# Recurrent attention with a rational feed-forward: the written order of all steps replaced, with some copies, products and half sums on other engines

## The chip, the core and the metric

One core of a Trainium2 chip runs the whole kernel. The metric is device time in microseconds (us) of one execution; lower is better. PE is the matrix engine (TensorE), DVE VectorE, ACT ScalarE, POOL GpSimd, SP the engine that mostly issues transfers. Each engine works through its own queue strictly in the order in which the kernel was written, and waits at an instruction whose inputs or buffers are not ready.

## The reference, cut to what matters

```
f = 1 / (1 + exp(-f_logit))                          # q, k, v, f_logit: 4 x 8 x 768 x 48
for t in range(768):
    state = f[:, :, t, :, None] * state + outer(k[t], v[t])
    y[:, :, t] = q[t] @ state                        # per batch and head
x = y as 3072 tokens x 384
h = x @ w_in                                         # 384 -> 2048
P = a0 + a1 h + a2 h^2 + a3 h^3
Q = 1 + |b0| |h| + |b1| h^2
out = (P / (Q + 1e-6)) @ w_out                       # 2048 -> 384
```

## The kernel before, in words

The 3072 tokens are cut into twelve units of 256 (four batches, three stretches of time). A unit goes through an attention part and a feed-forward part, and several units are under way at once.

Attention part of a unit. `ld` loads f, k, q (SP's queue) and v (POOL's queue). ScalarE takes exp and log of the gate (`ef`, L284; `ls`, L289). PE forms running sums (`cs`, L299 to L308). ScalarE takes their exp, once for q and once for k (`A`, L316), and a short one for the chunk decay (`ae`, L448). `xa` (L321) multiplies q (x = 0) or k (x = 1) with that into `qkp`, on VectorE or, with the letter p, on GpSimd. `T` (L335) transposes the products on PE into PSUM, and `Te` copies them into SBUF as T: on ScalarE with the letter s (L344), read as 1024 words of 32 bits, or on VectorE (L345), as 2048 of 16 bits. `sc` (L357) and `mk` (L365, VectorE) form masked scores; `ic`, `si` and `st` (L422, L432, L452) carry the state on; `yi` and `yb` (L377) form y. `ye` scales y into x, on ScalarE (L440) with a factor held in a register that `fr` (L278) loads, or on VectorE (L442).

Feed-forward part. `h` (L463) is a quarter of x @ w_in, four blocks of 128; `hy` (L480, ScalarE) brings it to SBUF. VectorE forms `sq` (h squared, L484), `ab` (the absolute value, L488), `p1`, `pm`, `p2` (L524, L534, L529). The sum z of the denominator is made by an adding transfer that POOL issues (`zd`, L510), by VectorE (`zv`, L506), or on PE (`u`, L496). The last sum of the numerator, into g, is likewise an adding transfer (`ta`, L538) or a half sum on VectorE (`tv`, L542). ScalarE takes the logarithm of the denominator (`lz` L514, or `ln` L501 out of PSUM) and exp of its negative (`ex`, L519) into qi; `gm` (L546) multiplies that into g; `o` (L555) is a quarter of g @ w_out for 128 tokens; `oe` (L562) copies it out of PSUM on ScalarE or VectorE and `so` (L571) stores it. The two last numbers of a feed-forward step are its range of the 16 blocks of 128.

What sets the order. ORDER (L19 to L94) is a written-out list of all steps; it is walked once, and each step appends its instructions to the queues of its engines. `@0` to `@3` names one of four PSUM slots of two banks each; a new tile in a slot waits until the old one has been read. `!x2` marks a step, and `^x2` lets a later step begin only behind the marked one; the loads of w_in (`wi`, L212) all carry `^w`, the mark of the fifth load of SP's queue, half of unit 0's q. Transfers have eight semaphores per issuing kind, used in turn: the ninth transfer of a kind waits on its queue until the first has landed. v 0 and v 1 are the first two of POOL's, the twelve pieces of w_in follow, so the ninth to the twelfth piece wait for the first to the fourth.

Of the kernel before, what the change touches and what calls it, by code (L numbers as in the profile page):

```python
# [29 lines left out]
yi 1 1 @0; hy 0 12 16; yb 1 2 4; yb 1 0 2; ls 3; ab 0 8 16; u 0 0 4 @3; ef 4; sq 0 8 16; ld 6 f; cs 3 @2; ld 5 f  # L30
ln 0 0 4; p1 0 0 16; T 2 @1; ye 1 s; ae 3; Te 2 s; h 1 4 8 @3; zv 0 8 16; ld 4 k; pm 0 0 16; u 0 4 8 @0; A 3 0
ld 4 q; si 2 0 @1; hy 1 4 8; ic 2; ln 0 4 8; ld 5 q; st 2 0; vm 3; h 1 8 12 @3; ld 4 v; p2 0 0 16; A 3 1; si 2 1
ls 4; sc 2 1 @0; st 2 1; wo 4 8; h 1 0 4 @2; hy 1 8 12; xa 3 0 !x3; ef 5; vm 2; mk 2 1; sc 2 0 @1
# [590 lines left out]
```

## Time and profile before

| what | value |
|---|---|
| three runs | 217.24, 218.63 and 219.75 us, median 218.63 |
| the profiled execution, its whole time | 217.03 us |
| its span, first to last instruction | 215.3 us |
| what lies around the span | 1.73 us |
| granted PE clock, mean | 0.995 |
| DMA queue of POOL / of SP, share of 16 engines | 70.3% / 35.4% |
| transfers, whole kernel | 44.22 MB |

In a row of groups stand line, engine, operation, output and input with their shapes and the count, then busy us and the mean ns of one, then the idle time ahead of them and what ended it. In a row of time stand start, duration, engine, line, operation and count. In a row of waits stand who waited for whom, the us in total, how often and the longest. In a row of stretches stand the stretch, its length and the busy time of each engine with the number of its instructions. Records of neighbouring instructions on one engine overlap a little, so the distance between two starts is shorter than a duration.

### The profile page before, as it was taken

The page shows a single profiled execution, that of the slowest core. Times are in us where ns is not written, and L with a number is a line of the kernel's source. Part 1 is how long each engine was busy: PE and PEld are TensorE (multiplying, and loading weights), DVE is VectorE, ACT ScalarE, POOL GpSimd, SP SyncE. Part 2 cuts the span into 40 slices and gives each one's busy share as a digit, 9 for nine tenths or more (in the row PEclk, how much of TensorE's full clock was granted, in tenths as well). Part 3 has the DMA queues.
Part 4 walks back from the last instruction along what each step waited for, and adds up shares of the span by engine and source line. Part 5 has one row for each costly group of instructions (what it writes and reads, how often), then busy time and mean ns, then how long its engine had stood idle before and what let it go on. Part 6 is the DMA issues. An engine that isn't in the chain of part 4 may idle for free.

```text
span 215.3 us, 6663 instructions
## 1 busy us (share of the span) xinstructions
PE 193.1 (90%) x2931; PEld 139.9 (65%) x2933; DVE 197.4 (92%) x195; ACT 190.1 (88%) x182; POOL 88.5 (41%) x101
## 2 busy tenths in 40 slices
PE   0396799989998999999989999999999999999991
PEld 0374577767874777775876875875885667765550
DVE  3199789999999999999999999999999999999961
ACT  2753499997999899999999999999999899999970
POOL 7174070734935418134447449371155303431100
PEclk9999999999999999999999999999999999999997
DMA  5999999999999999999998999999999998799865
GB/s 140 223 231 213 241 251 225 232 220 254 202 172 201 180 199 219 254 189 258 244 278 192 193 178 202 187 211 208 169 216 204 197 196 191 150 195 195 174 182 146
DMA packets 62557, 44.22 MB, mean 205 GB/s; under 512 B 51520, under 2 KB 57408, under 8 KB 62528
## 3 DMA queue, kind: packets, MB, share of 16 engines
q0 software_dynamic: 21264, 24.91, 70.3%
q1 hardware_dynamic: 40896, 18.78, 35.4%
q8 instruction: 23, 0.38, 0.7%
q10 hardware_dynamic: 368, 0.10, 0.3%
q14 instruction: 6, 0.05, 0.1%
HBM read 25.17 MB, written 4.72 MB: 139 GB/s over the span
## 4 chain that ended last, share of the span: by engine, by line
ACT 26%; PE 26%; DVE 24%; DMA 11%; issue 9%; SPq 1%; ACTq 0%; DVEq 0%
PE op L555 11%; PE hp L463 9%; ACT hy L480 8%; ACT qi L519 8%; DMA w_in_sb<-in_moe_w_in_dram 6%; DVE scm L365 5%; ACT lq L514 5%; DVE h L484 4%; DMA q<-in_q_dram 3%; DVE g L534 3%; PE y L377 3%; DVE z L506 2%; ACT A L316 2%; DMA out_dram<-osb 2%; DVE z L488 2%
## 5 line engine op out<-in xcount | busy, mean ns | idle before, releaser
L463 PE MATMUL hp<-x,w_in_sb 128*128 128x256 bf16 x576 | 68.0, 273 | 2.8 <-DMA w_in_sb<-in_moe_w_in_dram 1.0
L555 PE MATMUL op<-w_out_sb,g 128*128 128x384 bf16 x384 | 68.8, 326 | 0.7 <-ACT hy L480 0.4
L463 PEld LDWEIGHTS <-w_in_sb 128*128 128x128 bf16 x576 | 55.3, 98 | 13.1 <-issue 3.9
L480 ACT CAST hy<-hp 128x1024 bf16<-128x1024 f32 x48 | 48.1, 1046 | 5.0 <-PE hp L463 4.0
L555 PEld LDWEIGHTS <-g 128*128 128x128 bf16 x384 | 36.1, 98 | 23.8 <-issue 1.1
L519 ACT ACTIVATE qi<-lq 128x4096 bf16<-128x4096 f32 (+1 forms) x14 | 44.2, 3172 | 0.0
L514 ACT ACTIVATE lq<-z 128x2048 f32<-128x2048 bf16 x22 | 42.2, 1961 | 0.0
L510 POOL DMA_DIRECT2D z<-h x17 | 18.7, 1155 | 34.7 <-DVE z L488 16.8
L538 POOL DMA_DIRECT2D g<-hy x20 | 19.5, 1012 | 30.9 <-PE hp L463 9.6
L484 DVE TENSOR_TENSOR h<-hy 128x4096 bf16<-128x4096 bf16 (+1 forms) x14 | 29.3, 2090 | 2.5 <-ACT hy L480 2.5
L546 DVE TENSOR_TENSOR g<-g,qi 128x4096 bf16<-128x4096 bf16 (+2 forms) x19 | 28.0, 1496 | 0.9 <-ACT qi L519 0.8
L365 DVE TENSOR_TENSOR scm<-sc,mask 128x1024 bf16<-128x1024 f32 x24 | 28.6, 1211 | 0.0
L534 DVE TENSOR_TENSOR g<-g,h 128x4096 bf16<-128x4096 bf16 (+1 forms) x16 | 28.1, 1768 | 0.0
L316 ACT ACTIVATE A<-cs 128x768 f32<-128x768 f32 (+1 forms) x26 | 19.9, 786 | 1.6 <-PE cs L308 1.5
L321 POOL TENSOR_TENSOR qkp<-q,A 128x768 bf16<-128x768 f32 x7 | 12.7, 1820 | 16.7 <-DMA q<-in_q_dram 7.1
L299 PE MATMUL cs<-lsp,Ui 128*128 128x384 bf16 (+1 forms) x39 | 11.1, 344 | 9.1 <-ACT lsp L289 8.7
L284 ACT ACTIVATE f<-f 128x768 f32<-128x768 f32 (+1 forms) x13 | 10.4, 817 | 8.9 <-DMA f<-in_f_logit_dram 8.9
L529 DVE TENSOR_SCALAR hy<-hy,a_sb 128x4096 bf16<-128x4096 bf16 (+1 forms) x13 | 16.5, 1267 | 0.0
L524 DVE TENSOR_SCALAR g<-hy,a_sb 128x4096 bf16<-128x4096 bf16 x12 | 16.1, 1342 | 0.0
L488 DVE TENSOR_SCALAR z<-hy 128x4096 uint16<-128x4096 uint16 (+1 forms) x15 | 15.4, 1028 | 0.0
L335 PE MATMUL tp<-ident,qkp 128*128 128x128 bf16 x192 | 13.6, 227 | 1.5 <-DVE scm L365 1.5
L321 POOL TENSOR_TENSOR qkp<-k,A 128x768 bf16<-128x768 f32 x6 | 10.9, 1821 | 9.4 <-ACT hy L480 8.2
(77 smaller groups left out, 250.0 us busy)
## 6 DMA issues: line engine op xcount, KB each, us to landing
g<-hy POOLq DMA_DIRECT2D x20, 512.0 KB, 7.2
z<-h POOLq DMA_DIRECT2D x17, 512.0 KB, 9.0
f<-in_f_logit_dram SPq DMA_DIRECT2D x11, 384.0 KB, 8.5
k<-in_k_dram SPq DMA_DIRECT2D x11, 384.0 KB, 8.6
q<-in_q_dram SPq DMA_DIRECT2D x11, 384.0 KB, 7.1
out_dram<-osb SPq DMA_DIRECT2D x18, 192.0 KB, 5.7
v<-in_v_dram POOLq DMA_DIRECT2D x12, 192.0 KB, 8.5
w_out_sb<-in_moe_w_out_dram POOLq DMA_DIRECT2D x4, 384.0 KB, 7.7
```

The source lines that it names most:

```text
L316: nc.scalar.activation(t, src, AF.Exp, scale=1.0 if x else -1.0)
L321: i = (nc.gpsimd if eng == "p" else nc.vector).tensor_mul(s["qk"][:, x, :, hh, 0:D], s["qk"[x]][:, hh].rearrange("p h i d -> p i h d"), s[ ...
L365: return nc.vector.tensor_mul(t, s["sc", g].rearrange("s r a i t -> s (r a) (i t)"), mb)
L463: nc.tensor.matmul(t[:, m - m0, :].rearrange("f (j t) -> f j t", j=UB), w_in_sb[:, kk, m * P:(m + 1) * P], s["x"][:, :, kk, :], start=(kk ...
L480: nc.scalar.copy(fl(big(s, "hy"), m0, m1), fl(s["hp", m0], 0, m1 - m0))
L484: return nc.vector.tensor_mul(fl(big(s, "h2"), m0, m1), fl(big(s, "hy"), m0, m1), fl(big(s, "hy"), m0, m1))
L488: return nc.vector.tensor_scalar(fl(big(s, "z"), m0, m1).bitcast(U16), fl(big(s, "hy"), m0, m1).bitcast(U16), 0x7FFF, None, op0=ALU.bitwis ...
L514: nc.scalar.activation(fl(lq, m0, m1), fl(big(s, "z"), m0, m1), AF.Ln, scale=regs[2], bias=1.0 + 1e-6)
L519: nc.scalar.activation(fl(qi, m0, m1), fl(lq, m0, m1), AF.Exp, scale=-1.0)
L534: return nc.vector.tensor_mul(fl(big(s, "g"), m0, m1), fl(big(s, "g"), m0, m1), fl(big(s, "h2"), m0, m1))
L546: return nc.vector.tensor_mul(fl(big(s, "g"), m0, m1), fl(big(s, "g"), m0, m1), fl(qi, m0, m1))
L555: nc.tensor.matmul(s["op", g][:, j, 0:DM], big(s, "g")[:, m, C * j:C * j + C], w_out_sb[:, m, :], start=(s["on", j] == 1), stop=(s["on", j ...
```

## The change

ORDER is another list: 776 steps for 775. The matrix steps, loads, `hy`, `lz`, `mk`, `st` and `A` are as many as before; these differ:

| step | before | after |
|---|---|---|
| `Te` of a whole unit on ScalarE / VectorE | 8 / 3 | 10 / 1 |
| `xa` of a whole unit on GpSimd / VectorE | 13 / 9 | 15 / 7 |
| `oe` of two token blocks on ScalarE / VectorE | 8 / 3 | 10 / 1 |
| `ye` on ScalarE / VectorE | 11 / 1 | 12 / 0 |
| `zd` / `zv`, halves | 17 / 5 | 19 / 3 |
| `ta` / `tv`, halves | 20 / 4 | 17 / 6, and two quarters `tv` |
| `ex`, whole / half / quarter | 10 / 4 / 0 | 11 / 0 / 4 |
| `sq`, whole / half | 10 / 4 | 8 / 8 |
| `ab`, `pm`, `p2`, whole / half | 9 / 6, 8 / 8, 11 / 2 | 10 / 4, 9 / 6, 12 / 0 |
| `gm`, whole / half / quarter | 9 / 2 / 8 | 7 / 8 / 4 |

Of products GpSimd forms in sum two more, both of q; among those new on it is q of unit 1 (`xa 1 0 0 4 p ^x1`). Its place on POOL's queue is behind the last of the twelve w_in pieces and ahead of k of unit 2. On PE's queue `T 1`, `cs 2`, `sc 1 0` and `sc 1 1` stand directly ahead of the first quarter of h of unit 0, in this order; before, `T 1` stood further ahead, in front of `yi` and `yb` of unit 0, and the other three directly ahead of h. `ye 0` moves from VectorE to ScalarE and so waits for the register load `fr`, and that for the factors of `fa`, which VectorE now forms behind the first scores. The pieces of w_in come in another sequence, and the fourth of them is 192 KB where it was 96. SP's queue loads k of unit 2 as its eleventh transfer and q of unit 2 as its thirteenth; before they were the other way round. `oe` may also name GpSimd, which the list does not use.

The start of the list, where unit 0 reaches its feed-forward part, is before and after:

```diff
-ab_ b a; ld 0 f 2 4; cz 1; cu 1; ld 0 f 0 2; cz 0; ld 0 k 0 2; ci; ld 1 f; ld 0 v; ld 1 v; ld 0 q 2 4 !w
...
-T 0 0 2 @1; xa 0 1 2 4; A 1 0; wi 3 8 16 ^w; cm; wi 1 0 4 ^w; T 0 2 4 @0; fr
-ld 3 f; Te 0 0 2; wi 2 0 4 ^w; A 1 1; vm 1 v; si 0 0 @1; Te 0 2 4; sc 0 0 @2; xa 1 1; sc 0 1 @0; wi 3 4 8 ^w
-ic 0; xa 1 0; ld 2 k; ic 1; wi 3 0 4 ^w; mk 0 0; wi 2 8 16 ^w; ef 2; st 1 0; T 1 @2; wi 0 8 16 ^w; st 0 0; ls 2
-mk 0 1; si 0 1; si 1 1; yi 0 1 @0; st 1 1; yb 0 0 2; fb; yb 0 2 4; Te 1; ld 4 f; cs 2 @3; st 0 1; sc 1 0 @2
-A 2 0; ye 0 v !x2; sc 1 1 @1; A 2 1; mk 1 0; h 0 4 8 @0; ae 2; xa 2 0 0 4 p ^x2; mk 1 1; h 0 0 4 @3; hy 0 4 8
```

```diff
+wi 3 4 8 ^w; A 0 1 0 2; ld 2 f; vm 0; xa 0 1 2 4; wi 0 4 8 ^w; xa 0 1 0 2; T 0 2 4 @2; ae 1; ab_ a a
+wi 0 8 16 ^w; xa 0 0 0 2; wi 1 4 8 ^w; Te 0 2 4; ld 2 k; A 1 0; wi 1 0 4 ^w; T 0 0 2 @2; wi 2 0 4 ^w; A 1 1
...
+st 0 0 !x1; wi 0 0 4 ^w; mk 0 1; si 0 1; sc 0 0 @2; wi 2 8 16 ^w; st 1 0; yi 0 1 @0; mk 0 0; si 1 1
+wi 1 8 16 ^w; yb 0 2 4; ld 2 q; xa 1 0 0 4 p ^x1; st 1 1; yb 0 0 2; fa; ef 2; T 1 @2; fb; ls 2; st 0 1; fr
+cs 2 @1; Te 1 !x2; ye 0 s; ld 4 f; A 2 0; sc 1 0 @3; sc 1 1 @0; A 2 1; mk 1 0; h 0 4 8 @2; mk 1 1; h 0 0 4 @3
```

The end of the list is before and after:

```diff
-o 10 0 8 12; gm 11 0 4; ex 11 8 16; o 11 1 4 8 @1; oe 10 0 2 v; o 11 0 0 4 @3; so 10 0 2; o 11 0 4 8; oe 8 0 2 s
-gm 11 8 12; o 11 1 0 4; gm 11 12 16; so 8 0 2; o 11 0 8 12; o 11 0 12 16; o 11 1 8 12; oe 11 0 1 s; o 11 1 12 16
-so 11 0 1; oe 11 1 2 v; so 11 1 2 b
```

```diff
+o 10 0 8 12; gm 11 0 4; o 11 0 4 8 @1; ex 11 8 12; oe 10 0 2 v; o 11 1 0 4 @0; ex 11 12 16; o 11 1 4 8
+gm 11 8 12; so 10 0 2; o 11 0 0 4; oe 8 0 2 s; gm 11 12 16; o 11 0 8 12; so 8 0 2; o 11 0 12 16; o 11 1 12 16
+oe 11 0 1 s; o 11 1 8 12; so 11 0 1; oe 11 1 2 v; so 11 1 2 b
```

And the one line of code beside the list:

```diff
     def oe(n, j0, j1, eng="v"):
-        return (nc.scalar.copy if eng == "s" else nc.vector.tensor_copy)(
+        return {"s": nc.scalar.copy, "p": nc.gpsimd.tensor_copy, "v": nc.vector.tensor_copy}[eng](
```

More of the change, by code (lines that the diff above doesn't have):

```diff
@@ L30 @@
[L30 to L33, printed above, removed]
-xa 3 1 0 4 p ^x3; h 1 12 16 @3; hy 1 0 4; mk 2 0; ls 5; cs 4 @0; ta 0 0 8; tv 0 8 16; hy 1 12 16; ld 8 f; ld 5 k
@@ L90 @@
[L90 to L93 removed]
+ld 0 f 2 4; cz 2; cu 1; cz 3; cz 0; ld 0 k 0 2; ld 0 f 0 2; ci; ld 1 f; cu 0; ld 0 v; ld 0 q 2 4 !w; cm; cz 1
+ld 0 k 2 4; ld 1 v; ef 0 2 4; ld 0 q 0 2; ls 0 2 4; ab_ b a; cs 0 2 4 @0; ld 1 k; ef 0 0 2; ls 0 0 2; si 1 0 @1
```

126 lines of the change are left out of this document (65 added, 61 removed).

## The prediction

> **What bounds the kernel now.** I read the head of the page first, then the busy time in one long stretch, then the waits in it. The stretch runs from the start of the second `hy` of unit 0 (26.83) to the end of the last `ex` (207.46).
>
> ```profile
> span 215.3 us, 6663 instructions
> PE 193.1 (90%) x2931; PEld 139.9 (65%) x2933; DVE 197.4 (92%) x195; ACT 190.1 (88%) x182; POOL 88.5 (41%) x101
> ```
>
> ```profile
> 26.83:207.46 180.63, 174.65 (x2635) 126.80 (x2638) 177.86 (x144) 176.24 (x158) 77.26 (x74) 1.00 1.08 207
> ```
>
> ```profile
> DVE h L484 <- ACT hy L480: 2.5, 2, 2.1
> DVE g L546 <- ACT qi L519: 0.8, 1, 0.8
> ACT hy L480 <- PE hp L463: 4.0, 7, 1.8
> ```
>
> In 180.63 us VectorE works 177.86, ScalarE 176.24 and PE 174.65. VectorE is the bound: its 2.8 idle us are one wait of 2.1 at the very start and little else. ScalarE is idle 4.4, mostly in `hy` behind PE, PE 6.0. So three engines stand within 2% of each other: what is taken from VectorE can bring a few us at most, and what is put on ScalarE soon costs. Ahead of the stretch lies a start bound by transfers, behind it a chain from `ex` to the last store.
>
> **The change on VectorE and ScalarE.** Prices are distances between starts, because records overlap:
>
> ```profile
> 153.61 1.07 ACT L344 COPY T<-tp 128x1024 f32<-128x1024 f32 x1
> 154.50 0.88 ACT L562 COPY osb<-op 128x768 f32<-128x768 f32 x1
> 155.19 2.02 ACT L480 CAST hy<-hp 128x1024 bf16<-128x1024 f32 x2
> ```
>
> ```profile
> 73.45 1.21 DVE L345 COPY T<-tp 128x2048 bf16<-128x2048 bf16 x1
> 74.58 0.54 DVE L452 TENSOR_TENSOR state<-sv,ae 128x384 bf16<-128x384 f32 x1
> ```
>
> ```profile
> L519 ACT ACTIVATE qi<-lq 128x4096 bf16<-128x4096 f32 x10 | 36.5, 3652 | 0.0
> L440 ACT ACTIVATE x<-y 128x768 bf16<-128x768 f32 x11 | 9.1, 824 | 0.7 <-PE y L377 0.7
> L519 ACT ACTIVATE qi<-lq 128x2048 bf16<-128x2048 f32 x4 | 7.7, 1972 | 0.0
> L506 DVE TENSOR_TENSOR z<-z,h 128x2048 bf16<-128x2048 bf16 x5 | 6.1, 1211 | 0.0
> L321 DVE TENSOR_TENSOR qkp<-q,A 128x768 bf16<-128x768 f32 x4 | 3.8, 946 | 0.0
> L562 DVE COPY osb<-op 128x768 f32<-128x768 f32 x2 | 1.9, 946 | 0.0
> L546 DVE TENSOR_TENSOR g<-g,qi 128x4096 bf16<-128x4096 bf16 x9 | 20.5, 2280 | 0.0
> L546 DVE TENSOR_TENSOR g<-g,qi 128x2048 bf16<-128x2048 bf16 x2 | 2.3, 1209 | 0.0
> L442 DVE TENSOR_SCALAR x<-y,sig 128x768 bf16<-128x768 f32 x1 | 1.0, 1008 | 0.0
> ```
>
> A T copy costs ScalarE 154.50 - 153.61 = 0.89 and VectorE 74.58 - 73.45 = 1.13; an output copy costs ScalarE 0.69. So records overlap by about 0.18 on ScalarE and 0.08 on VectorE.
>
> ScalarE gains 2 T copies (1.78), 2 output copies (1.38) and one x (0.824 less overlap and a little, 0.70). Its exp pieces go from 10 whole and 4 halves (44.41 by records) to 11 whole and 4 quarters; a quarter, half a half's slope off, is 1.972 - 0.840 = 1.13, so 44.70, less one more overlap: +0.1. Together **+4.0**. The x of unit 0 falls ahead of the stretch, so **+3.3 within it**.
>
> VectorE loses 2 T copies (2.26), 2 products of q (2 x 0.87), 2 output copies (2 x 0.87), one x (0.92), 2 halves of z (2 x 1.13). It gains 2 half sums (2 x 1.13) and 2 quarter sums (half of that and a start, 2 x 0.60); of its other steps, cut elsewhere, one piece fewer remains, and a cut costs 2 x 1.209 - 2.280 = 0.14. Together **-5.6**; the product of q 1 and the x of unit 0 were ahead of the stretch, so **-3.8 within it**.
>
> GpSimd's two added products can hold VectorE up:
>
> ```profile
> 27.50 1.81 POOL L321 TENSOR_TENSOR qkp<-q,A 128x768 bf16<-128x768 f32 x1 [7.12 <-DMA q<-in_q_dram]
> 27.88 2.52 DVE L484 TENSOR_TENSOR h<-hy 128x2048 bf16<-128x2048 bf16 x1 [2.12 <-ACT hy L480]
> 32.39 1.21 DVE L484 TENSOR_TENSOR h<-hy 128x2048 bf16<-128x2048 bf16 x1
> ```
>
> The same `sq` took 1.21 alone and 2.52 beside a product, ending 1.2 behind it. Each new product costs VectorE between 0 and 1.3; I take 0.3, as most of the thirteen leave no such record. POOL's transfers go from 37 adding ones to 36, SP's loads stay; in the middle they are covered, POOL being busy 77 of 180.63.
>
> So the busy sums of the stretch become ScalarE 176.2 + 3.3 = 179.5, PE 174.7 as before (no matrix step changes), VectorE 177.9 - 3.8 + 0.6 = 174.7. The bound passes to ScalarE, 1.1 short of the old length. What waits does it keep? At least 0. At most the 4.4 of today, if they come from PE's order. Added up along each queue with these prices, PE in the new list is 1.4 us or more ahead of every `hy` from unit 2 on, where in the old one it was level or behind in many; I take 0.5. **The stretch: 180.0** (179.5 to 183.9).
>
> **The start.** Here the change moves q of unit 1 from VectorE, where it ran early, to POOL behind the twelve w_in pieces.
>
> ```profile
> 15.73 0.95 DVE L321 TENSOR_TENSOR qkp<-q,A 128x768 bf16<-128x768 f32 x1
> 20.90 1.22 DVE L345 COPY T<-tp 128x2048 bf16<-128x2048 bf16 x1
> ```
>
> ```profile
> 10.62 4.45 POOL L212 DMA_DIRECT2D w_in_sb<-in_moe_w_in_dram  x8 [1.91 <-DMA q<-in_q_dram]
> 16.41 1.19 POOL L212 DMA_DIRECT2D w_in_sb<-in_moe_w_in_dram  x2 [1.34 <-DMA w_in_sb<-in_moe_w_in_dram]
> 19.22 1.16 POOL L212 DMA_DIRECT2D w_in_sb<-in_moe_w_in_dram  x2 [1.62 <-DMA w_in_sb<-in_moe_w_in_dram]
> ```
>
> ```profile
> 17.86 1.05 PE L335 MATMUL tp<-ident,qkp 128*128 128x128 bf16 x16 [1.48 <-DVE scm L365]
> 22.17 0.88 PE L357 MATMUL sc<-T 48*64 48x128 bf16 x32
> 24.00 2.79 PE L463 MATMUL hp<-x,w_in_sb 128*128 128x256 bf16 x24 [0.95 <-DMA w_in_sb<-in_moe_w_in_dram]
> 26.83 1.01 ACT L480 CAST hy<-hp 128x1024 bf16<-128x1024 f32 x1 [0.30 <-PE hp L463]
> ```
>
> Today h of unit 0 waits for w_in, until 24.00; the scores of unit 1 were done at 23.05. POOL's last piece is issued by 19.22 + 1.16 = 20.38, held there by waits for earlier pieces to land. In the new list the twelfth waits for a fourth piece twice as large; the first and third let go 19.22 - 16.41 = 2.81 apart, 1.4 a piece, so it costs 0 to 1.4 more; I take 0.5: 20.9. Then one after the other: the product 1.81 (22.7), the transposes of unit 1, 1.05 (23.8), VectorE's copy 1.22 (25.0), the scores 0.88 (25.9). PE's queue has h of unit 0 behind those scores, and `cs 2` too, though x of unit 0 is ready by then (its factors end some 20.5, its copy under 22). So h starts at 25.9 instead of 24.0, and the second `hy` at 25.9 + 2.83 = **28.8** instead of 26.83. Bounds: 26.8, if POOL comes free early enough for w_in to stay the last to come; 29.7 with the full 1.4. The new order of the first f, k and q loads makes the first products some 0.5 us earlier; that goes into the wait on POOL. Behind the product on POOL stand k of unit 2 and the loads of v 2 and v 3, all 2 us later and all covered until VectorE's first feed-forward work, itself later by nearly as much less what the held `sq` lost.
>
> **The end.**
>
> ```profile
> 205.55 1.91 ACT L519 ACTIVATE qi<-lq 128x2048 bf16<-128x2048 f32 x1
> 207.49 1.29 DVE L546 TENSOR_TENSOR g<-g,qi 128x1024 bf16<-128x1024 bf16 x2 [0.78 <-ACT qi L519]
> ```
>
> ```profile
> 200.35 10.67 PE op L555 x64
> 211.05 0.56 DVE f L562
> ```
>
> Today 215.3 - 207.46 = 7.84 follow the last `ex`: two `gm` (1.29), matmuls until 211.05, the copy, the store of 3.7. With quarters only one `gm` (0.68, half of 1.29 and an overlap) is left behind the last `ex`, then three fours of matmuls (12 x 10.67 / 64 = 2.0), copy 0.56, store 3.7: 7.0. But PE runs its last 64 matmuls without a gap (10.67), and may be behind: then 7.8 as today. I take **7.4**.
>
> **Sum.** 28.8 + 180.0 + 7.4 = 216.2, against 215.3: +0.9. The profiled execution took 217.03 for its 215.3, so 217.9. The runs' median, 218.63, lies 1.6 above that execution; the middle of all four times (217.03, 217.24, 218.63, 219.75) is 217.9, and with +0.9 I put the median at **218.8**.
>
> **Rivals.** *Slower: ScalarE keeps its waits.* VectorE now waits for ScalarE (`gm` behind an `ex` of 3.65), and `mk` and `st` behind that `gm` come late, then y, x and h, and ScalarE stands in `hy` after all. For it speaks that VectorE, with 5 us in hand, can no longer run ahead; against it PE's lead. With the 4.4 of today and the end as today: 28.8 + 183.9 + 7.8 = 220.5, +5.2, about 223; it decides (over 1%, 2.2 us) from 1.8 us of ScalarE waits on.
>
> *Faster: the relief of VectorE counts in full.* POOL is free early (26.8), ScalarE runs unbroken (179.5), the end is short (7.0): 213.3, -2.0, and past -2.2 as soon as 0.2 of ScalarE's recorded work was short waits between its records; about 215.6 for the median. For it speaks that ScalarE has been idle 4.4; against it the w_in waits on POOL, which stand in the rows. A rule also points this way: the Trainium skill, page "Perfetto Trace Analysis", section "Identifying the Most-Contended Engine", holds that matmul busy time misjudges the headroom of the matrix engine, that weight-load busy time is a better measure (65% here, against 90%), and that the engine with the highest occupancy is to be relieved first. By that rule PE does not bind, the busiest engine falls from VectorE's 197.4 to ScalarE's 194.1, and the span by 3.3, to 212.0, 1.5%. The trace agrees in that VectorE has the highest share; ScalarE's wait for PE in `hy` (4.0) speaks against PE's headroom.
>
> *The change does not do what it says:* the products hold VectorE by the full 1.3 each. Then it has 176.7 busy, still under ScalarE's 179.5: no other time, only less slack.
>
> **Chances.** Forecast (within 1%) 0.49; waits kept, 0.33; relief in full, 0.18. About 1% is what a measurement of this kernel can tell from no change. The forecast's own range is 216.6 to 221.0. The range, 214.8 to 222.8, reaches from the faster rival into the slower. So faster by over 1% 0.18, within 0.49, slower 0.33.
>
> **What would show it.** Right: ScalarE has the highest busy time, near 194, VectorE near 192; the second `hy` of unit 0 starts near 28.8, with POOL's first product near 20.9 and PE idle ahead of the transposes of unit 1; VectorE waits in `gm` for qi. Wrong: POOL's product before 17, `hy` waiting over 2 us in sum behind PE, or x late behind y.

## The result, and the profile after

| | before | after |
|---|---|---|
| five runs of each, median (lowest to highest), us | 217.68 (216.48 to 219.75) | 225.20 (224.29 to 225.42) |
| span of the profiled execution, us | 215.3 | 222.8 |

The ratio is 1.0341, interval 1.0289 to 1.0393: the change made the kernel 3.4% slower, outside the predicted range. The head of the page of after:

```profile
span 222.8 us, 6655 instructions
PE 198.3 (89%) x2933; PEld 142.9 (64%) x2933; DVE 191.4 (86%) x189; ACT 193.4 (87%) x188; POOL 91.9 (41%) x102
```

The busy times came out as forecast: ScalarE 193.4 (194 forecast), VectorE 191.4 (192). No engine has more work to do than was reckoned, so the 6.6 us by which the span exceeds the forecast are waiting, and the next view must say where. Two stretches of after follow: the first 40 us, and from the start of unit 0's second `hy` to the end of the last `ex` (stretch, length, then busy PE, PEld, DVE, ACT, POOL, granted clock, in which a time without any clock record counts as 1.00):

```profile
0.00:40.00 40.00, 26.11 (x394) 19.26 (x395) 19.93 (x51) 18.16 (x29) 18.12 (x33) 1.00 1.17 206
35.15:214.22 179.07, 173.83 (x2640) 126.22 (x2639) 173.44 (x140) 178.91 (x165) 75.13 (x71) 1.00 1.06 196
```

The same first 40 us of before:

```profile
0.00:40.00 40.00, 27.09 (x477) 20.54 (x479) 29.83 (x59) 25.19 (x38) 16.47 (x31) 1.00 1.17 218
```

In the long stretch ScalarE is busy 178.91 of 179.07: it is the bound, as predicted, and stands idle 0.16. In the first 40 us it works 18.16 where it worked 25.19. Its idle time there is 21.84 against 14.81, and those 7.03 us are nearly all of the 7.5. By the prediction's three terms:

| term | before | forecast | after | after less forecast |
|---|---|---|---|---|
| start of the second `hy` | 26.83 | 28.8 | 35.15 | +6.35 |
| to the end of the last `ex` | 180.63 | 180.0 | 179.07 | -0.93 |
| from there to the end | 7.84 | 7.4 | 8.58 | +1.18 |
| span | 215.3 | 216.2 | 222.8 | +6.6 |

The chain that ended last, in the part of after that leads to the second `hy` (start, us, what):

```profile
10.60 15.54 DMA f<-in_f_logit_dram
26.17 0.85 ACT f L285
27.04 0.85 ACT lsp L290
27.89 0.04 issue
27.94 1.44 PE cs L300 x4
29.38 0.19 PE cs L306 x8
29.60 1.00 PE sc L358 x28
30.60 4.53 PE hp L464 x24
35.15 1.01 ACT hy L481
```

The prediction's chain ran from POOL's last w_in piece through the product of q 1. The real one begins with a load on SP's queue, f of unit 2, which took 15.54 us to land. ScalarE's exp of it (`ef 2`) stood in ScalarE's queue ahead of unit 0's x, and its running sums (`cs 2`) in PE's queue ahead of unit 1's scores and of h of unit 0. ScalarE's rows of after say the same (start, busy, and in brackets the idle time ahead and what ended it):

```profile
26.17 0.84 ACT L285 ACTIVATE f<-f 128x768 f32<-128x768 f32 x1 [10.44 <-DMA f<-in_f_logit_dram]
27.98 0.81 ACT L441 ACTIVATE x<-y 128x768 bf16<-128x768 f32 x1
33.31 1.01 ACT L481 CAST hy<-hp 128x1024 bf16<-128x1024 f32 x1 [2.10 <-PE hp L464]
35.15 1.01 ACT L481 CAST hy<-hp 128x1024 bf16<-128x1024 f32 x1 [0.83 <-PE hp L464]
```

and this is the first of them in before:

```profile
19.12 0.84 ACT L284 ACTIVATE f<-f 128x768 f32<-128x768 f32 x1 [5.00 <-DMA f<-in_f_logit_dram]
```

One instruction, waiting 10.44 us in one program and 5.00 in the other, and 7.05 later. POOL's queue in after:

```profile
3.07 1.99 POOL L208 DMA_DIRECT2D v<-in_v_dram  x2
8.48 1.12 POOL L213 DMA_DIRECT2D w_in_sb<-in_moe_w_in_dram  x2 [3.42 <-DMA q<-in_q_dram]
10.66 3.33 POOL L213 DMA_DIRECT2D w_in_sb<-in_moe_w_in_dram  x6
19.04 0.56 POOL L213 DMA_DIRECT2D w_in_sb<-in_moe_w_in_dram  x1 [0.60 <-DMA w_in_sb<-in_moe_w_in_dram]
24.02 1.81 POOL L322 TENSOR_TENSOR qkp<-q,A 128x768 bf16<-128x768 f32 x1 [4.42 <-DVE state L453]
```

v goes out 0.87 later than before (3.07; it was 2.20), because POOL first forms the constant of `cu 0`. The loads of w_in start 2.14 earlier (8.48; they started at 10.62), because their mark, half of unit 0's q, lands earlier. POOL was free at 19.60, 1.3 sooner than the forecast, yet the product began at 24.02. The row names VectorE's state, but in the list the product waits for another, earlier one (`st 0 0`); it also needs q of unit 1, whose last part landed at 23.88 by the trace's landing records (one for each of the sixteen parts of a load). A second profile of after names that load outright:

```profile
20.47 1.81 POOL L322 TENSOR_TENSOR qkp<-q,A 128x768 bf16<-128x768 f32 x1 [1.54 <-DMA q<-in_q_dram]
```

What the transfers did from 10 to 20 us, by queue (q1 is SP's, q0 POOL's; packets, MB, share of the 16 engines), in before:

```profile
q1 hardware_dynamic: 4125, 1.55, 76.5%
q0 software_dynamic: 670, 0.75, 46.6%
```

and in after:

```profile
q0 software_dynamic: 1213, 0.98, 63.8%
q1 hardware_dynamic: 3212, 1.21, 62.3%
```

Together 2.30 and 2.19 MB: no more came in, but the shares changed. SP's queue carried 0.34 MB less in that time, nearly one whole load of 384 KB; POOL's carried 0.23 more.

### The profile page after: what moved, and what is told of

It is laid out like the page before. It is cut to its first block, busy times and chain, and to the rows that moved or that the text cites. A ratio compares the mean times of both kernels' runs of the same rounds, so it can differ in the third digit from the quotient of the medians.

```text
span 222.8 us, 6655 instructions
## 1 busy us (share of the span) xinstructions
PE 198.3 (89%) x2933; PEld 142.9 (64%) x2933; DVE 191.4 (86%) x189; ACT 193.4 (87%) x188; POOL 91.9 (41%) x102
## 3 DMA queue, kind: packets, MB, share of 16 engines
q0 software_dynamic: 21120, 24.38, 66.9%
## 4 chain that ended last, share of the span: by engine, by line
ACT 62%; issue 15%; PE 9%; DMA 7%; SPq 4%; DVE 1%; ACTq 0%
ACT hy L481 18%; ACT lq L515 12%; ACT qi L520 11%; DMA f<-in_f_logit_dram 7%; ACT A L317 5%; SPq L208 4%; PE op L556 4%; ACT f L285 3%; ACT lsp L290 3%; ACT x L441 3%; PE hp L464 3%; ACT T L345 2%; ACT osb L563 2%; ACT lq L502 1%; PE cs L300 1%
## 5 line engine op out<-in xcount | busy, mean ns | idle before, releaser
L464 PE MATMUL hp<-x,w_in_sb 128*128 128x256 bf16 x576 | 69.7, 277 | 1.7 <-ACT x L441 1.3
L464 PEld LDWEIGHTS <-w_in_sb 128*128 128x128 bf16 x576 | 56.8, 99 | 12.6 <-issue 2.9
L481 ACT CAST hy<-hp 128x1024 bf16<-128x1024 f32 x48 | 50.8, 1122 | 2.9 <-PE hp L464 2.9
L515 ACT ACTIVATE lq<-z 128x2048 f32<-128x2048 bf16 x22 | 44.6, 2059 | 0.0
L539 POOL DMA_DIRECT2D g<-hy x17 | 16.8, 1064 | 43.4 <-DVE hy L530 17.0
L547 DVE TENSOR_TENSOR g<-g,qi 128x2048 bf16<-128x2048 bf16 (+2 forms) x19 | 28.5, 1507 | 2.7 <-ACT osb L563 1.7
L366 DVE TENSOR_TENSOR scm<-sc,mask 128x1024 bf16<-128x1024 f32 x24 | 28.7, 1214 | 2.2 <-PE sc L358 2.0
L485 DVE TENSOR_TENSOR h<-hy 128x2048 bf16<-128x2048 bf16 (+1 forms) x16 | 28.1, 1757 | 0.0
L322 POOL TENSOR_TENSOR qkp<-q,A 128x768 bf16<-128x768 f32 x9 | 16.5, 1831 | 27.0 <-ACT lq L515 8.2
L336 PEld LDWEIGHTS <-qkp 128*128 128x128 bf16 x192 | 12.5, 105 | 6.6 <-POOL qkp L322 3.2
L530 DVE TENSOR_SCALAR hy<-hy,a_sb 128x4096 bf16<-128x4096 bf16 x12 | 16.1, 1338 | 0.0
```

Source lines behind the costliest of these rows:

```text
L336: nc.tensor.transpose(t[:, x, i, p, :], s["qk"][:, x, i, 2 * p:2 * p + 2, :].rearrange("t h d -> t (h d)"), ident)
L366: return nc.vector.tensor_mul(t, s["sc", g].rearrange("s r a i t -> s (r a) (i t)"), mb)
L464: nc.tensor.matmul(t[:, m - m0, :].rearrange("f (j t) -> f j t", j=UB), w_in_sb[:, kk, m * P:(m + 1) * P], s["x"][:, :, kk, :], start=(kk ...
L481: nc.scalar.copy(fl(big(s, "hy"), m0, m1), fl(s["hp", m0], 0, m1 - m0))
L485: return nc.vector.tensor_mul(fl(big(s, "h2"), m0, m1), fl(big(s, "hy"), m0, m1), fl(big(s, "hy"), m0, m1))
L515: nc.scalar.activation(fl(lq, m0, m1), fl(big(s, "z"), m0, m1), AF.Ln, scale=regs[2], bias=1.0 + 1e-6)
```

## The experiments

Four causes were set against each other; the recorded expectations call them T1 to T4. **Loads** (T1): w_in starts earlier and v later, and the late f 2 and q 1 on SP's queue hold the start. **Product** (T2): the prediction's own cause, q 1 behind the twelve w_in pieces on POOL. **Order of the queues** (T3): f 2's steps stand ahead of unit 0's h, so any late load is paid there. **PE's rate** (T4): 24 matmuls of h took 4.53 us in after and 2.79 in before.

All measured values stand in one table: the ratio to before with its 95% interval, the span, the start of w_in, of `ef 2` (it begins as f 2 lands, but for e4, where f 2 landed at 25.81 and `ef 2` stood behind `hy`), and of the second `hy`, and ScalarE's idle time in the first 40 us (40 less its busy time in that stretch).

| kernel | ratio (interval) | span | w_in | `ef 2` | `hy` | idle |
|---|---|---|---|---|---|---|
| before | 1 | 215.3 | 10.62 | 19.12 | 26.83 | 14.81 |
| after | 1.0341 (1.0289 to 1.0393) | 222.8 | 8.48 | 26.17 | 35.15 | 21.84 |
| e1_w_later | 1.0261 (1.0218 to 1.0303) | 220.2 | 11.39 | 24.40 | 32.13 | 18.80 |
| e2_q1_vector | 1.0330 (1.0286 to 1.0373) | 221.1 | 8.27 | 25.92 | 33.51 | 20.19 |
| e3_before_w_early | 1.0276 (1.0233 to 1.0318) | 220.6 | 8.86 | 25.07 | 32.61 | 20.03 |
| e4_h0_first | 1.0476 (1.0430 to 1.0522) | 225.7 | 9.31 | 30.62 | 29.71 | 24.03 |
| e5_pe_busy | 1.0260 (1.0171 to 1.0349) | 221.9 | 8.23 | 26.04 | 33.83 | 20.51 |
| e6_v_first | 1.0180 (1.0090 to 1.0269) | 220.1 | 9.61 | 24.98 | 32.54 | 19.22 |
| e7_before_v_later | 1.0316 (1.0225 to 1.0407) | 221.1 | 9.61 | 25.40 | 33.24 | 20.65 |
| e8_before_q1_gpsimd | 1.0036 (0.9998 to 1.0074) | 216.9 | 11.06 | 20.99 | 28.85 | 16.23 |
| e9_v_first_w_later | 1.0205 (1.0139 to 1.0271) | 219.5 | 11.57 | 19.01 | 32.07 | 18.75 |
| e10_all_three | 1.0217 (1.0157 to 1.0278) | 221.9 | 11.77 | 18.75 | 29.88 | 16.97 |
| e11_old_start | 1.0082 (1.0046 to 1.0118) | 217.1 | 10.70 | 21.65 | 29.17 | 16.59 |
| e12_old_start_short_end | 1.0066 (1.0032 to 1.0100) | 217.8 | 10.54 | 22.01 | 29.60 | 17.01 |
| e13_h0_all_first | 1.0250 (1.0208 to 1.0293) | 221.5 | 8.20 | 27.09 | 29.6 | 20.12 |
| r1_before | | 216.0 | 11.13 | 19.68 | 29.14 | 16.54 |
| r2_after | | 221.5 | 9.43 | 25.29 | 33.88 | 20.56 |
| r3_cross | | 220.7 | 10.95 | 23.37 | 32.29 | 19.67 |
| r4_v_later | | 221.1 | 9.66 | 25.20 | 33.82 | 21.24 |

**Span less that idle time** is 199.5 to 201.7 in every row but one (e10, 204.9). In the six rows with before's middle and end (before, e3, e7, e8, r1, r4) it is 200.3 on average, in the twelve others without e10 201.1. By its making this number is all of ScalarE's work and its idle time behind 40 us, so it says where the time goes and not why. Read so, the changed middle and end are worth no gain, rather a loss of 0.8, and the programs differ by how long ScalarE stands idle at the start. The second `hy` alone misleads: in e4, e13 and r1 it is early or late with no matching change of the span. Two profiles of one program differ by 0.0 (e7), 0.7 (before), 1.3 (after) and 3.6 (e11) in span, so smaller differences are read from the ratios.

### What of before's list, changed, makes after's loss

**e3**, before with the mark that lets w_in go moved to an earlier load:

```diff
-ld 1 f; ... ld 0 q 2 4 !w
+ld 1 f !w; ... ld 0 q 2 4
```

> The kernel before, with the mark for w_in put on f of unit 1, an earlier load of SP's queue, so that w_in's pieces can start near 7.5 to 8.5 instead of 10.6. T1, the loads: SP's loads that follow lose their share as in after; q of unit 1 lands at 18 to 24 instead of 15.7, f of unit 2 at 22 to 26 instead of 19.1, the second hy of unit 0 starts 2 to 6 us later than 26.83, and the time is 1 to 3% above before. T3 (queue order) or T2 (product on GpSimd): w_in earlier only helps h of unit 0, which waited for w_in until 24.0; hy at 25 to 27, time within 1% of before.

w_in 1.76 earlier, f 2 at ScalarE 5.95 later, ratio 1.0276. No work was added or taken. Letting w_in go earlier is enough to make the greater part of the loss.

**e7**, before with the constant `cu 0` ahead of v on POOL's queue, as in after. Nothing else is moved.

```diff
-ci; ld 1 f; ld 0 v; ld 1 v; ld 0 q 2 4 !w; ld 0 q 0 2; cu 0
+ci; ld 1 f; cu 0; ld 0 v; ld 1 v; ld 0 q 2 4 !w; ld 0 q 0 2
```

> The kernel before, with one step moved: the mask Ui (three GpSimd operations, 0.87 us in all) is made ahead of the loads of v 0 and v 1, as in after, so that these are issued at 3.07 instead of 2.20. T1, the loads: that shift alone decides the start. The mark (q of unit 0, second half) then lands at 8.2 to 9.3 instead of 10.34, w_in's pieces go out at once, and q of unit 1 and f of unit 2 lose their share: f of unit 2 lands at 22 to 26 instead of 19.1, the second hy of unit 0 starts 2 to 6 us later than 26.83, time 1 to 3% above before. Rival, the loads' own order on SP's queue (k ahead of f of unit 0, k of unit 2 ahead of q of unit 2) or the other steps of after did it: v 0.87 us later is hidden, hy at 26.8 to 27.5, time within 0.5% of before.

Rows of e7, POOL's and then ScalarE's:

```profile
3.08 1.99 POOL L207 DMA_DIRECT2D v<-in_v_dram  x2
9.61 4.44 POOL L212 DMA_DIRECT2D w_in_sb<-in_moe_w_in_dram  x8
25.40 0.84 ACT L284 ACTIVATE f<-f 128x768 f32<-128x768 f32 x1 [11.29 <-DMA f<-in_f_logit_dram]
33.24 1.01 ACT L480 CAST hy<-hp 128x1024 bf16<-128x1024 f32 x1 [0.30 <-PE hp L463]
```

v 0.88 later, w_in 1.01 earlier, f 2 6.28 later, ratio 1.0316: one constant moved past two transfers on a queue gives, within the intervals, the whole loss of the change. Not all of it is the wait for f 2: PE's granted clock reads 0.50 from 17.47 to 31.13 here, and from the first sums of unit 2 to the second `hy` it took 6.08 us, where the same steps at the full rate take 0.87 + 0.57 + 2.83 = 4.3. From 10 to 20 us its two queues stand as in after:

```profile
q0 software_dynamic: 1447, 1.07, 67.7%
q1 hardware_dynamic: 3181, 1.20, 54.3%
```

**r1, r2, r4 and r3** profile before, after, e7 and e11 a second time, since a landing can be chance.

> The kernel before, profiled a second time, to see how much of the landing times is the execution's. If they belong to the program: f of unit 2 lands at 18.6 to 19.6, the second hy at 26.3 to 27.4. If a start like this is open to chance by a few us, f of unit 2 lands anywhere from 18 to 23, and the cross, which has the same first loads, is no proof of anything but chance.

> The kernel after, profiled a second time. If the late landings belong to the program: f of unit 2 at 25 to 27, second hy at 33.5 to 35.5. If they are chance: f of unit 2 below 23.

> The kernel before with v 0 and v 1 behind the mask Ui, profiled a second time: by the loads, w_in begins near 9.6, f of unit 2 lands at 24.5 to 26, the second hy comes at 32.5 to 34 again. By chance: f of unit 2 below 22.

> The cross, profiled a second time: its first loads are those of before, yet f of unit 2 landed at 21.65 and the second hy came at 29.17. By chance: this time 19 to 20 and 27. By something that belongs to the program: 21 to 22.5 and 28.8 to 29.8 again.

`ef 2` began at 19.12 and 19.68 in before, at 26.17 and 25.29 in after, at 25.40 and 25.20 in e7. The late f 2 belongs to the program. The cross of e11 scatters: 21.65 and 23.37, and its span 217.1 and 220.7; the execution of r3 (222.39 us) was longer than all ten timed runs of e11 (218.00 to 221.36).

**e8**, before with the product of q 1 on POOL behind the w_in pieces and `T 1` behind y of unit 0: the step that the prediction priced, done alone.

```diff
-xa 1 0; ...; st 1 0; T 1 @2; ...; wi 0 8 16 ^w; st 0 0; ...; yb 0 2 4; Te 1
+st 1 0; ...; wi 0 8 16 ^w; xa 1 0 0 4 p; st 0 0; ...; yb 0 2 4; T 1 @2; Te 1
```

> The kernel before, with the step that the prediction charged for the start, and nothing else of the change: the product of q of unit 1 on GpSimd behind the twelve pieces of w_in, and the transposes of unit 1 behind y of unit 0, where after has them. T2, the prediction's step: GpSimd is free at 20.4, the product ends at 22.2, transposes at 23.3, copy 24.5, scores 25.4, so h starts at 25.4 instead of 24.0 and the second hy at 28.2 (26.83 before); span 216 to 217, time 0.4 to 0.9% above before. T1 says nothing against this, only that it is not what cost 7.5 us: loads land as in before, f of unit 2 at 19 to 20. If hy comes at 30 or later, the product was worth more than the prediction said.

Its row on POOL:

```profile
20.83 1.82 POOL L321 TENSOR_TENSOR qkp<-q,A 128x768 bf16<-128x768 f32 x1
```

The product came at 20.83 (20.9 forecast), h of unit 0 began at 26.03 (25.9 forecast; 24.00 and 24.64 in the two profiles of before), and the time rose by 0.36%, as +0.9 us would have it, with an interval that reaches to zero. The step was priced rightly where it stands; it was the small part. That the second `hy` at 28.85 meets the forecast (28.8) says less: in r1 it came at 29.14 with no product moved. f 2 was 1.3 to 1.9 later than in before as well.

### What of after's list, changed back, returns it

**e1**, after with w_in let go later (mark on `ld 0 k 2 4`), and **e2**, after with q 1's product on VectorE:

```diff
-ld 0 q 2 4 !w; cm; cz 1; ld 0 k 2 4
+ld 0 q 2 4; cm; cz 1; ld 0 k 2 4 !w
```

> The kernel after, with the mark for which all w_in pieces wait put one load later on SP's queue (k instead of q of unit 0, second half). T1, the loads: in after the mark landed at 8.2 instead of 10.3, w_in's large packets got onto the 16 engines 2 us earlier and SP's small-packet loads lost their share: q of unit 1 landed at 23.9 (15.7 before) and f of unit 2 at 26.1 (19.1). So here w_in starts near 12, f of unit 2 lands at 19 to 22, the second hy of unit 0 starts at 28.8 to 30 instead of 35.15, and the span is 216 to 218 instead of 222.8. T2, the reason of the prediction (the product of q of unit 1 stands on GpSimd behind the w_in pieces): later pieces hold the product as much or longer, hy at 35 or later, span 222 or more. T3, the queue order alone: hy stays within 1 us of 35.

```diff
-ld 2 q; xa 1 0 0 4 p ^x1; st 1 1
+ld 2 q; xa 1 0; st 1 1
```

> The kernel after, with the product of q of unit 1 back on VectorE; nothing else moves. T2, the reason of the prediction: this product behind the w_in pieces is what costs the start, so hy of unit 0 comes 2 us or more earlier and the span is 219.5 to 221. T1, the loads: the product waits for q of unit 1, which lands at 23.9, and h of unit 0 waits on PE's queue for cs of unit 2 and so for f of unit 2, which lands at 26.1: hy stays at 34.5 to 35.2 and the span within 1 us of 222.8.

e1 takes 2.6 from the span, and f 2 still comes at 24.40: a later w_in alone is not enough. By its landing records the middle one of that load's sixteen parts came at 18.34, the fifteenth at 21.59, the last at 24.38, so what is left is a fifteenth part 2.5 later than before's (19.07) and a last one 2.8 behind that. In e2 f 2 is as late as in after, the span is 1.7 shorter, and the ratio's interval lies almost wholly within that of after: with the product gone from POOL's path hardly anything is won, as long as f 2 is late.

**e6**, after with v back ahead of `cu 0`, and the last adding transfer made a half sum on VectorE:

```diff
-ld 1 f; cu 0; ld 0 v; ...; ld 0 k 2 4; ld 1 v
+ld 1 f; ld 0 v; ld 1 v; cu 0; ...; ld 0 k 2 4
-gm 10 8 16; ta 11 8 16
+gm 10 8 16; tv 11 8 16
```

> The kernel after with two edits that are read at different places. Start: the loads of v 0 and v 1 go out ahead of the mask Ui, at 2.20 as in before. T1, the loads: the mark then lands near 10, w_in's pieces begin at 10.3 to 10.6, f of unit 2 lands at 19 to 22 instead of 26.14, and the second hy of unit 0 starts at 28.5 to 31 instead of 35.15. Rival: the loads' own order on SP's queue or the steps' order costs the start, hy stays at 33 or later. End: the last half of the sum into g of unit 11 is formed on VectorE, which stood idle 1.7 us there, not by an adding transfer, which was issued at 208.08 and landed 6.7 later, behind the last exp; the end behind the last exp should be 7.3 to 7.9 instead of 8.58. If the wait was for the output copy on ScalarE, as the profile's row names it, the end stays at 8.3 or more. Together 216 to 218 of span.

f 2 at 24.98: v alone is not enough either. The ratio fell to 1.0180 all the same: the product on POOL came at 19.12 instead of 24.02 and the second `hy` 2.61 earlier, of which f 2 is 1.19. The end took 220.1 - 211.67 = 8.43, against 8.58.

**e9**, v back as in e6 and w_in later as in e1, with the end as in after:

```diff
-ld 1 f; cu 0; ld 0 v; ld 0 q 2 4 !w; cm; cz 1; ld 0 k 2 4; ld 1 v
+ld 1 f; ld 0 v; ld 1 v; cu 0; ld 0 q 2 4; cm; cz 1; ld 0 k 2 4 !w
```

> The kernel after with both edits of the loads together: v 0 and v 1 ahead of the mask Ui, and the mark for w_in one load later. Each alone left f of unit 2 late (24.4 and 25.0): with the mark later v's small packets stood in the way from 8 to 14, with v first the mark landed at 9.3 and w_in began at 9.6. T1, the loads: together w_in begins near 11 and v is out of the way by 10, as in the kernel before, so f of unit 2 lands at 19.5 to 21.5, the second hy starts at 29 to 30.5 and the span is 216.5 to 218, what the prediction's own start (28.8) gives with the measured end. Rival: something in the order of SP's queue that neither edit touches keeps f of unit 2 late; it lands at 24 or later, hy at 32 or later.

Rows of e9, of ScalarE, POOL and PE:

```profile
19.01 0.84 ACT L285 ACTIVATE f<-f 128x768 f32<-128x768 f32 x1 [4.19 <-DMA f<-in_f_logit_dram]
22.72 1.82 POOL L322 TENSOR_TENSOR qkp<-q,A 128x768 bf16<-128x768 f32 x1
24.59 1.04 PE L336 MATMUL tp<-ident,qkp 128*128 128x128 bf16 x8 [3.41 <-POOL qkp L322]
```

Both together bring f 2 back to before's time (18.75 in e10, which has the same loads), so the order of SP's own loads, which stayed as in after, did not keep it late. Now the second limit shows: with w_in later, POOL reaches the product at 22.72, PE idles 3.41 for it, and the second `hy` is at 32.07; the steps of PE from there on ran for the most part at a granted clock of 0.50 (23.69 to 30.51). The prediction's cause binds only once the loads do not. The ratio is still 1.0205: with f 2 back in time most of the loss is paid at another place of the start.

**e10**, e9 with q 1 on VectorE and e6's end:

```diff
-xa 1 0 0 4 p ^x1
+xa 1 0
-gm 10 8 16; ta 11 8 16
+gm 10 8 16; tv 11 8 16
```

> The kernel after with every cause that the study has put a price on taken out: v first, w_in's mark one load later, the product of q of unit 1 on VectorE again, and the last half sum into g of unit 11 on VectorE. Expected: second hy at 27 to 29, stretch to the end of the last exp 179 as in after, end 7.8: span 214 to 216, time from 1% below to level with the kernel before. If the new order of the middle costs something that the start hid, the stretch grows to 181 or more and the span stays at 217.

The start is almost won (`hy` 29.88, idle 16.97), yet the ratio stays at 1.0217: ScalarE now waits behind the start as well. The stretch behind the start in e10:

```profile
40.00:60.00 20.00, 16.80 (x342) 11.89 (x344) 15.76 (x17) 16.10 (x17) 12.24 (x12) 0.83 1.03 203
```

ScalarE works 16.10 of 20 there (20.00 in after). Of the 3.90 idle, 1.98 are a wait for f of a later unit at 43.22 and 1.53 one for transposes of PE at 50.65, where the granted clock reads 0.50 (45.24 to 52.07).

**e11** joins before's list up to the product of k 2 with the rest of after (PSUM slots renamed); its first steps:

```diff
-ld 0 f 2 4; cz 2; cu 1; cz 3; cz 0; ld 0 k 0 2; ld 0 f 0 2; ci; ld 1 f; cu 0; ld 0 v; ld 0 q 2 4 !w; ...
+ab_ b a; ld 0 f 2 4; cz 1; cu 1; ld 0 f 0 2; cz 0; ld 0 k 0 2; ci; ld 1 f; ld 0 v; ld 1 v; ld 0 q 2 4 !w; ...
```

> A cross: the list of before up to the product of k of unit 2 (its loads, its start, its four quarters of h of unit 0), and from there all remaining steps in the order of after, with their engines. It tells whether the loss lies in the start alone. If so, the second hy is at 26.8 to 27.3, the stretch from there to the end of the last exp takes 179 to 180.5 as in after, the end 8.4 to 8.6: span 214.3 to 216.3, level with before (215.3) or up to 0.5% under it. Rival: the new order of the middle needs the late start, because the loads that follow (f of units 4 and 5, w_out) run into each other as in the kernel with all three causes taken out, where ScalarE stood waiting for f at 41 to 43; then the stretch grows to 182 or more and the span to 218 or more.

**e12** is e11 with e6's half sum and the copy of unit 10 behind a `gm`:

```diff
-ta 11 8 16; ...; oe 10 0 2 v; ...; gm 11 8 12; so 10 0 2
+tv 11 8 16; ...; gm 11 8 12; oe 10 0 2 v; so 10 0 2
```

> The cross, and at the end two edits: the last half sum into g of unit 11 on VectorE instead of an adding transfer, and VectorE's output copy of unit 10 behind the third gm quarter of unit 11 instead of ahead of it. With the sum on VectorE alone the end was 8.43 for 8.58, as PE then was the one behind; with the third gm 0.9 earlier PE starts its last matmuls earlier, and the end should be 7.6 to 8.0. If the start alone is the loss: span 213.5 to 215.3, time 0 to 1% under before. If the rival of the cross holds, 217.5 or more.

The old start takes most of the loss away: 1.0082 and 1.0066. What is left of it agrees with the 0.8 us of the table and the scatter of f 2 (21.65 and 22.01 here). From the second `hy` to the end of the last `ex` e11 takes 179.54 us and e12 179.57 (179.07 in after). The end of e12 took 8.63 (7.6 to 8.0 expected; 8.39 in e11): its two edits there won nothing. No kernel here beat before.

### Order of the queues, and PE's rate

**e4**, after with x of unit 0, its first two quarters of h and their `hy` ahead of `T 1`, `ef 2`, `ls 2`, `cs 2` and the scores of unit 1; **e13**, the stronger form: q 1 on VectorE, x of unit 0 ahead of `ef 2`, all four quarters of h ahead of unit 1's scores.

```diff
-fa; ef 2; T 1 @2; fb; ls 2; st 0 1; fr; cs 2 @1; Te 1 !x2; ye 0 s; ...; h 0 4 8 @2; mk 1 1; h 0 0 4 @3; hy 0 4 8
+fa; fb; st 0 1; fr; ye 0 s; h 0 4 8 @2; h 0 0 4 @3; hy 0 4 8; hy 0 0 4; T 1 @2; ef 2; ls 2; cs 2 @1; Te 1 !x2
```

> The kernel after, with x of unit 0, the first two quarters of h of unit 0 and their hy put ahead of the transposes of unit 1 and of exp, log and sums of f of unit 2, on ScalarE and PE; loads as in after. T3, the queue order: y of unit 0 was done at 22 and its factors at 22.8, but x waited at 27.98 behind exp and log of f 2, and h behind cs of unit 2. So x comes at 23 to 24, the second hy at 28 to 30 instead of 35.15, and the span at 217 to 219.5. If the late landings hold the start in any order (T1 in its hard form: the later steps of units 1 and 2 then leave ScalarE idle by as much), the span stays at 221 or more although hy comes early.

```diff
-xa 1 0 0 4 p ^x1; ...; ef 2; T 1 @2; fb; ls 2; st 0 1; fr; cs 2 @1; Te 1 !x2; ye 0 s; ld 4 f; A 2 0; sc 1 0 @3 ...
+xa 1 0; ...; T 1 @2; fb; st 0 1; fr; Te 1 !x2; ye 0 s; ef 2; ls 2; ld 4 f; h 0 4 8 @0; h 0 0 4 @3; cs 2 @1 ...
```

> The kernel after with its loads as they are, the product of q of unit 1 on VectorE, and the start ordered by what is there first: x of unit 0 ahead of exp of f of unit 2 on ScalarE, all four quarters of h of unit 0 ahead of the scores of unit 1 on PE, and on VectorE the first absolute value and square ahead of the masked scores. T3, the queue order: the late f of unit 2 then holds nothing of unit 0; second hy at 27.5 to 29.5 (33.51 with the product on VectorE alone), VectorE's first feed-forward work at 28 to 30 instead of 36.2, span 217 to 219 (221.1 with the product alone). Rival: as in the first try of that kind, what is won for unit 0 is given back at unit 1, whose scores, y and x come later: span 220 or more.

Both had the second `hy` some 5.5 us earlier than after, yet e4 was the slowest kernel of all (1.0476), and e13 (1.0250) won less than 1%. PE in e4:

```profile
33.34 0.64 PE L358 MATMUL sc<-T 48*64 48x128 bf16 x32
36.22 4.17 PE L464 MATMUL hp<-x,w_in_sb 128*128 128x256 bf16 x24 [2.24 <-DVE scm L366]
```

The first half of h was early and the second half waited for unit 1's scores to leave the PSUM slot, behind the same late work. Moving what waits gains nothing while what it waits for stays late: unit 1 pays.

**e5**, after with 14 matmuls into a spare PSUM tile ahead of and behind `T 1` (added work; nothing reads it):

```diff
-fa; ef 2; T 1 @2; fb
+fa; ef 2; wm 0 8 @1; T 1 @2; wm 0 6 @1; fb
```

> The kernel after with 14 added matmuls of 128 x 384 on PE that only write a spare PSUM tile: 8 ahead of the transposes of unit 1, 6 behind them, where PE stood idle 2.9 and 1.0 us. T4: PE ran at half its rate from 18 to 37 because it stood idle in between (24 matmuls of h in 4.53 us, before in 2.79; 1.44 for the sums of unit 2, before 0.87), though the granted clock of the profile reads 1.00 there. Then h of unit 0 takes 2.8 to 3.0 a half, and the second hy starts at 32 to 33.5 instead of 35.15; span 220 to 221. Rival: the slow matmuls wait for something else (w_in, PSUM): they stay at 4.5, hy at 35 or later.

The chain of e5:

```profile
27.80 0.81 PE cs L300 x4
28.61 0.18 PE cs L306 x8
28.79 0.03 PE cs L309
28.82 0.57 PE sc L358 x32
29.40 4.41 PE hp L464 x24
```

Sums and scores went back to 0.81 and 0.57 (1.44 and 1.00 in after), but h stayed at 4.41, and the ratio's interval overlaps that of after: no gain is shown. PE's rate is a real part of the chain, 4.53 - 2.79 = 1.74 in h and 0.63 + 0.43 in front of it, but this cure reached only the smaller one.

Where the profile has records of the granted clock, the rate goes with it. In r1 it falls within h of unit 0:

```profile
22.00:25.37 3.37, 1.91 (x50) 1.52 (x49) 3.37 (x5) 1.59 (x3) 0.00 (x0) 1.00 1.17 228
25.37:28.78 3.41, 3.41 (x18) 2.37 (x17) 0.54 (x1) 1.01 (x1) 2.46 (x2) 0.50 1.13 273
28.78:31.66 2.88, 2.88 (x29) 2.39 (x27) 1.47 (x2) 2.52 (x3) 1.12 (x2) 1.00 1.23 232
```

The matmuls of h start 109 ns apart up to 25.3, 213 ns apart up to 28.7, then 109 again. In e5 the row reads 0.50 from 29.45 to 32.86, in which the distance is 213 ns as well. After's 1.00 of the first 40 us does not say that its clock was full: the clock records of that profile begin only at 34.24 (at 15.10 in before), and its matmuls of h stand 213 ns apart up to 34.1 and 109 from 34.3 on.

## Why the prediction was wrong, point by point

- **Busy sums and the bound: right.** ScalarE 178.91 in the stretch (179.5 forecast), VectorE 173.44 (174.7), PE 173.83 (174.7). The bound passed to ScalarE.
- **The waits that ScalarE keeps: right, and better than taken.** 0.16 where 0.5 was taken, and the stretch took 179.07 (180.0 forecast), 179.54 with before's start in e11; the slower rival, with 4.4 of waits kept, did not happen. The kernel got slower by a cause that no rival named.

Waits of after in the long stretch (who for whom, us, times, longest):

```profile
DVE z L489 <- ACT hy L481: 3.6, 1, 3.6
DVE g L547 <- ACT qi L520: 1.0, 2, 0.5
ACT hy L481 <- PE hp L464: 0.8, 1, 0.8
```

ScalarE's 4.0 behind PE became 0.8 (the second `hy` itself, at the very edge), and VectorE now waits for it, as foreseen, though in `gm` only 1.0.

- **The relief of VectorE: right in size, worth nothing.** Its busy time fell by 6.0. (Its `sq` beside the product, in the prediction's row, ended 30.40 - 29.31 = 1.1 behind it and not 1.2.) But ScalarE's work rose by 3.3 (190.1 to 193.4; 4.0 forecast), and behind the first 40 us its idle time fell by no more than 2.8 (215.3 - 190.1 - 14.81 = 10.4, now 222.8 - 193.4 - 21.84 = 7.6): work took the place of waits. The faster rival fails with it. The Trainium skill, page "Perfetto Trace Analysis", section "Identifying the Most-Contended Engine", would relieve the engine with the highest occupancy first. That was done here, the highest fell from 197.4 to 193.4, and this trace does not bear the rule out; it is no test of the rule alone, as the start was changed with it.
- **The start: the step that failed.** The prediction took the landings on SP's queue as those of before and let only POOL's queue move (it counted that "SP's loads stay", and the new order of the first loads "goes into the wait on POOL"). It priced the moved product, its place and its length rightly, as e8 shows (20.83 against 20.9 for the product, 26.03 against 25.9 for h). It did not ask what the earlier start of w_in and the later start of v do to SP's transfers beside them. In its place e3 and e7 show that moving w_in, or v and with it w_in, by one or two us costs f 2 six, with no change of work, and e9 that setting both back returns f 2 to 19.01. The prediction also took PE's durations at the rate of before. Of the missed 6.35 us, 30.60 - 25.9 = 4.7 is the late end of unit 1's scores, behind f 2 and q 1, and 4.55 - 2.83 = 1.7 is h at half the clock for most of its length. That the late f 2 alone makes after's loss is not shown: e9 has it back and is still 2.05% slower. What is shown is that shifts of these loads alone make such a loss (e3, e7), and that the start of before takes most of it away (e11, e12).
- **x of unit 0 ready early, "its copy under 22": wrong.** Its factors were ready at 22.70 + 0.73 = 23.43, but its copy ran at 27.98, behind `ef 2` and `ls 2` on ScalarE's queue. The prediction looked at when its inputs come (its factors at 20.5), not at what stands ahead of it.
- **Its sign of being wrong, `hy` waiting over 2 us in sum behind PE: it did,** 2.10 and 0.83, both in the start.
- **The end: 7.4 forecast, 8.58 measured.** The tail of after:

```profile
208.08 0.86 POOL L539 DMA_DIRECT2D g<-hy  x1 [6.01 <-DVE g L535]
212.22 2.00 ACT L520 ACTIVATE qi<-lq 128x1024 bf16<-128x1024 f32 x2
214.90 1.29 DVE L547 TENSOR_TENSOR g<-g,qi 128x1024 bf16<-128x1024 bf16 x2 [1.72 <-ACT osb L563]
215.65 2.77 PE L556 MATMUL op<-w_out_sb,g 128*128 128x384 bf16 x16 [0.97 <-DVE g L547]
```

The last two `gm` start 0.68 behind the last `ex` (214.22) and together, so nothing of the quarters was won. The row names the copy `osb`, which ended at 214.91; by its landing the adding transfer issued at 208.08, there at about 214.8, is what they waited for; the second profile of after (r2) names it. e6 takes it away: `gm` follows at once, and then PE is the limit.

```profile
210.35 5.37 PE L556 MATMUL op<-w_out_sb,g 128*128 128x384 bf16 x32 [0.82 <-DVE g L547]
211.68 1.28 DVE L547 TENSOR_TENSOR g<-g,qi 128x1024 bf16<-128x1024 bf16 x2
215.76 0.56 DVE L563 COPY f<-op 128x384 f32<-128x384 f32 x1 [2.80 <-PE op L556]
```

So 8.43 instead of 8.58. PE is behind, as the prediction's upper case had it (PE "may be behind", 7.8 us), but by more; the transfer of 6.7 us on the path, which it left out, is worth 0.15 of the 1.18.

**What stays open.** Why 1 to 2 us in the start of two transfers cost f 2 six: by the landing records the middle one of its sixteen parts moves by 4 to 5 (17.64 in before, 22.76 in after, 21.40 in e7), and the last part comes 1.5 to 6 behind the middle one; no run moved only the middle or only the last. That POOL's packets take SP's share fits the bytes of the queues, but no run changed the size or the number of those packets. Why the cross of e11, with before's first loads, has f 2 at 21.65 and 23.37 instead of 19. That e9 and e10, with f 2 in time, are still 2% slower is read from the waits of one profile each. And what makes the granted clock fall stays open too.

## What to carry to other kernels

Where the start is bound by transfers, list every load under way beside a moved one, and ask of each how late it lands and which queue it heads; a constant moved past two transfers cost, within the intervals, as much as this whole change. Then add up the idle time of the engine that bounds the rest: here span less ScalarE's idle time in the first 40 us was one number, 199.5 to 201.7, and told more than any single instruction's start. A relief of a busy engine was worth nothing here, where waits turned into work of the next one. And where the profile's clock row reads 1.00, see whether there is a record behind it, and look at the distance of the matmuls.

## What the runs showed of the hardware that was not expected

**The bytes of two queues came to much the same sum, and the shares moved.** From 10 to 20 us the total is 232 GB/s in before, 219 in after and 229 in e7, while SP's part goes 1.55, 1.21, 1.20 MB and POOL's 0.75, 0.98, 1.07. SP's packets there are of some 380 bytes (1.21 MB / 3212), POOL's of some 740 to 1120. The Trainium skill, page "DMA: Bandwidth & Descriptors", section "Queues, rings and completion order", says that each transfer engine takes turns between the queues it has work for, a packet at a time. The shares agree with that in direction, as with more of POOL's packets waiting SP's small ones would get fewer turns; no trace here shows the turns themselves, nor that the profile's packets are the page's. The page gives no size for it; here it is 22% of SP's bytes.

**The last part of a load decides, and it can be far behind.** f 2 of after: middle part at 22.76, last at 26.14; q 1: 16.55, fifteenth 19.33, last 23.88. The same page, section "Why a DMA increments its semaphore by 16 and not by 1", says that the sixteen engines finish a transfer independently and the waiter needs them all. These records agree.

**The granted clock halves in the start, and a 1.00 can stand for no record.** h of unit 0 took 4.53 / 24 = 189 ns a matmul in after and 2.79 / 24 = 116 in before. Where there are clock records, matmuls of h stand 213 ns apart at 0.50 and 109 at 1.00 (r1, e5); after's, 213 apart up to 34.1, lie ahead of its first record. The Trainium skill, page "TensorE: Matmul & The Clock Gate", section "Part 1: The HAM clock gate", has PE's clock fall to half after an idle window of about 3.4 us and rise again after a busy one. The records agree in the half and in the length: the stretches at 0.50 in the start are of 3.41 us (r1, e5, e6, e11), 6.83 (r2, e9), 10.24 (e3) or 13.65 (e7, r4). They do not agree in that PE would have to stand idle for a whole window: in the 3.37 us ahead of the fall in r1 it worked 1.91, in the 3.42 ahead of that in e5 1.65, while at the same time in before, with 2.32 of 3.42, the clock did not fall. In e5 the fall came 1.65 us after work had begun again (27.80 and 29.45).
